# Reordering the first FFN1 group, two transposes, output copies and one unit's loads in a fused retention and FFN kernel

## The chip, the cores and the metric

One core of one Trainium2 chip. The metric is the device time of one execution in microseconds (us), lower is better. Where a mean granted TensorE clock matters it is given as a share of full speed.

## The reference, cut to what matters

```python
scores = scale * np.matmul(q, k.transpose(0, 1, 3, 2))     # 8 batches, 8 heads, 576 x 64
ret = scores * Dmat                                        # decay gamma_h ** (i - j), causal
attn = np.matmul(ret, v)                                   # -> x, 4608 tokens x 512
h = x @ w_in                                               # 512 -> 2048
g = np.where(h > 0.0, h, np.exp(np.minimum(h, 0.0)) - 1.0) # ELU
out = g @ w_out                                            # 2048 -> 512
```

## The kernel before

The engines go by short names: PE does the matmuls (TensorE), DVE is VectorE, ACT ScalarE, POOL GpSimd. A line such as L349 is a line of the kernel whose profile is shown; in a changed kernel the same code can stand a few lines lower.

Tokens are cut into 36 units of 128, and units into groups: the first group is units 0 to 2, then single units 3, 4 and 5, then larger groups. For a unit, `turn` transposes its queries and keys on PE (until unit 12; later ones by DMA) and copies them out on DVE and ACT; `scores` multiplies them; `masks` applies the causal mask on DVE; `inter`, `state` and `intra` (together the product) make the unit's output, and `put_x` copies it out of PSUM on DVE into the FFN input `xt`. FFN1 and FFN2 are the matmuls with `w_in` and `w_out`. For a group, FFN1 makes 16 tiles (for a single unit four share a PSUM bank, and "tile" then means the four). Each tile `ph` goes through three engines before its PSUM bank is free: `e` (exp, ACT), `m` (POOL), `g` (DVE).

PSUM, the memory that PE writes its results to, is the tight resource. The Trainium skill ("PSUM — Partial Sum Buffer", Specifications (TRN2)) gives 8 banks of 512 fp32 values per partition. This kernel uses all 8: 3 for `ph` (`h`), 1 for `pm` (`m`), 2 for scores and transposes (one two-bank tile, tag `sc`), 1 for products (`o`), 1 for the state.

```python
    def turn(u, bank=None, keys_on_v=False):
        ...
            else:
                both = ps_s.tile([P, 2, 2, HP, P], BF16, name="tr", tag="sc")   # two banks, one tile
                ps = [both[:, c, 0] for c in range(2)]
            ...                                                                 # 8 transposes on PE
            nc.vector.tensor_copy(t[:, c_v], ps[c_v])
            nc.scalar.copy(t[:, 1 - c_v], ps[1 - c_v])

    def stretch(u, ahead=True):            # the steady state, from unit 5 on
        ...
        scores(u + 1); inter(u); state(u); intra(u)      # shortened
        last = GROUPS[group_of[u][0]][-1] == u
        if last:
            put_x(u)
        if ahead:
            masks(u + 1)
        if not last:
            put_x(u)
        state_out(u)

    def finish(n=0):                       # puts the g's that are n slots old on DVE
        while late and late[0][0] <= slot[0] - n:
            _, gt_, ph, m, _ = late.pop(0)
            nc.vector.scalar_tensor_tensor(gt_, ph, 0.0, m, ALU.max, ALU.min)

    def tick():                            # after every FFN1 tile and every quarter of an FFN2 tile
        slot[0] += 1
        finish(3)
    ...
    load_w_in(1)                           # POOL issues these loads, in this order
    scale_v(1)
    load_qk(3)
    load_v(3, queue=nc.gpsimd)
    scale_v(2)
    load_w_in(2)
    load_w_in(3)
    load_w_out(0, 0, 8)
    load_w_out(0, 8, 16)
    load_w_out(1, 0, 16)
    dummy(2)
    for u in range(2):
        scores(u)
        masks(u)
        ...
        dummy(3)                           # keeps PE at work while it waits
        turn(u + 1, h, True)
        product(u)
        dummy(2)
    ...
    for n in range(2):
        ffn1_part(0, n, 0, 2)              # tiles 0 to 3 of units 0 and 1, ahead of unit 2
    product(2)
    for n in range(2, 4):
        ffn1_part(0, n, 0, 2, m if n == 3 else None)
    for n in range(4):
        ffn1_part(0, n, 2, 3)              # their part for unit 2
        f1(0, n)                           # e, m; g three slots later
    for n in range(4, 16):
        f1(0, n, m if n % 4 == 3 else None)
        if n == 5:
            turn(3)
        if n == 7:
            scores(3)
            masks(3, 0)
            scale_v(3)
        if n == 8:
            masks(3, 1)
        if n == 10:
            product(3)
    for n in range(4):
        f1(1, n, m if n == 3 else None)
        if n == 0:
            load_v(4, nc.vector)
        if n == 1:
            load_qk(4)
    finish()
    ...                                    # then FFN2 of units 0 to 3 in halves, turns 4 to 6
```

In these traces each engine runs its instructions in the order of the program text. The build adds the waits between engines.

## Time and profile before

| | before |
|---|---|
| time, median of 6 runs | 316.31 us (315.92 to 316.67) |
| span of the profiled run | 314.4 us |
| PE busy | 306.8 us, 98% |
| DVE, ACT, POOL busy | 55%, 42%, 64% |

The page of the kernel before: its busy times and the chain that ended last.

```profile
span 314.4 us, 7538 instructions
PE 306.8 (98%) x3020; PEld 173.9 (55%) x3020; DVE 172.7 (55%) x279; ACT 131.0 (42%) x243; POOL 200.9 (64%) x288
...
PE 89%; DVE 3%; DMA 3%; POOL 2%; issue 1%; ACT 0%; DVEq 0%; POOLq 0%; ACTq 0%
```

PE bounds the kernel and hardly ever stops. What can still be removed is in the view of waits of PE (columns: total us, times, longest):

```profile
PE dum L407 <- DVE warm L120: 1.2, 1, 1.2
PE ph L349 <- DVE g L316: 1.2, 1, 1.2
PE tr L194 <- DMA qkn<-in_k_dram: 0.8, 1, 0.8
PE pmh L390 <- DVE g L316: 0.3, 1, 0.3
PE sc L210 <- DVE rv L83: 0.2, 1, 0.2
PE tr L194 <- DVE pt L222: 0.2, 1, 0.2
```

This view hides the ends of matmuls that are still in the pipeline, so waits below read larger. They are start-to-start times of neighbouring matmuls minus the time the moving columns take: 1.33 us at 20.63 (FFN1 tile 4 of the first group waits for tile 0's bank), 0.44 at 37.8 (an FFN2 half waits for a bank), 0.31 at 57.55 and 0.33 at 69.91 (turns 7 and 9 wait for a mask), 0.24 at 113.34.

The stretch of the first group in the PE timeline of the kernel before (columns: start, length, engine, line, operation, tiles; in brackets idle time and what ended it):

```profile
20.63 1.46 PE L349 MATMUL ph<-xt,w_in_sb 128*128 128x384 bf16 x8 [1.16 <-DVE g L316]
21.93 0.61 PE L194 MATMUL tr<-ident,qkn 128*128 128x128 bf16 x8
22.38 1.46 PE L349 MATMUL ph<-xt,w_in_sb 128*128 128x384 bf16 x8
23.77 0.42 PE L210 MATMUL sc<-qkT 64*64 64x128 bf16 x16
24.12 2.14 PE L349 MATMUL ph<-xt,w_in_sb 128*128 128x384 bf16 x12
26.19 0.41 PE L238 MATMUL o<-qkT,sb 64*64 64x128 bf16 x8
```

After the one wait at 20.63, turn 3 (`tr`), FFN1 tiles, scores (`sc`) and product (`o`) follow without a gap. The same view of DVE and ACT has turn 3's copies at 22.58 to 23.00 (DVE) and 23.03 to 23.62 (ACT): the second starts 0.03 us after the first, although ACT was free from 22.68.

### The profile page before, as it was taken

To read this page: it belongs to the slowest core of one execution; us is meant where nothing else is said; L and a number is where in the kernel's file an instruction comes from. 1 tells how busy PE (TensorE), PEld (TensorE's weight loads), DVE (VectorE), ACT (ScalarE), POOL (GpSimd) and SP (SyncE) were. 2 spreads that over 40 slices of the span, in tenths; PEclk is the share of its full clock that TensorE was granted. 3 is DMA by queue.
4 is the path that set the end of the run, shared out by engine and by line. 5 is a ranking of instruction groups with operands and counts; after the bars stand their busy time and mean duration, and the time that the engine had idled before them with its cause. 6 is when DMAs were issued, how large, how long until landed. Compare 5 with 4: busy or idle time off the path is not lost.

```text
span 314.4 us, 7538 instructions
## 1 busy us (share of the span) xinstructions
PE 306.8 (98%) x3020; PEld 173.9 (55%) x3020; DVE 172.7 (55%) x279; ACT 131.0 (42%) x243; POOL 200.9 (64%) x288
## 2 busy tenths in 40 slices
PE   8889999999999999999999999999999999999995
PEld 3466888777665555555455444444444444444444
DVE  4658434757765656656655655555555555434300
ACT  4446314345434444343444444344444444344411
POOL 7977993968987788697777666766664433333300
PEclk9999999999999999999999999999999999999999
DMA  9999999996999999999999999999996200000111
GB/s 155 191 206 198 159 215 191 189 151 58 132 120 197 132 121 185 142 113 189 105 166 116 133 134 133 136 134 133 136 133 85 67 35 35 34 33 33 69 67 68
DMA packets 149235, 39.55 MB, mean 126 GB/s; under 512 B 137616, under 2 KB 145168, under 8 KB 149200
## 3 DMA queue, kind: packets, MB, share of 16 engines
q0 software_dynamic: 79264, 13.64, 56.7%
q1 hardware_dynamic: 67920, 23.14, 39.0%
q10 hardware_dynamic: 2016, 2.29, 2.3%
q8 instruction: 23, 0.38, 0.5%
q14 instruction: 12, 0.10, 0.1%
HBM read 36.70 MB, written 9.44 MB: 147 GB/s over the span
## 4 chain that ended last, share of the span: by engine, by line
PE 89%; DVE 3%; DMA 3%; POOL 2%; issue 1%; ACT 0%; DVEq 0%; POOLq 0%; ACTq 0%
PE ph L349 38%; PE pm L374 33%; PE pmh L390 5%; PE sc L210 4%; DMA w_in_sb<-in_moe_w_in_dram 3%; PE o L272 3%; PE st L255 2%; PE o L238 2%; PE dum L407 2%; PE tr L194 2%; DVE pt L222 1%; DVE g L316 1%; DVE xt L285 1%; POOL qkn L94 1%; POOL m L356 1%
## 5 line engine op out<-in xcount | busy, mean ns | idle before, releaser
L356 POOL TENSOR_SCALAR m<-e 128x512 bf16<-128x512 f32 (+1 forms) x156 | 90.9, 586 | 94.2 <-ACT e L354 91.9
L349 PE MATMUL ph<-xt,w_in_sb 128*128 128x512 bf16 (+3 forms) x816 | 143.2, 313 | 1.4 <-DVE g L316 1.2
L316 DVE SCALAR_TENSOR_TENSOR g<-ph,m 128x512 bf16<-128x512 f32 (+1 forms) x156 | 99.6, 647 | 80.8 <-POOL m L356 79.4
L354 ACT ACTIVATE e<-ph 128x512 f32<-128x512 f32 (+1 forms) x156 | 87.7, 565 | 125.0 <-PE ph L349 123.4
L374 PE MATMUL pm<-w_out_sb,g 128*128 128x512 bf16 x496 | 125.6, 379 | 0.0
L349 PEld LDWEIGHTS <-w_in_sb 128*128 128x128 bf16 x816 | 69.8, 98 | 54.8 <-issue 2.1
L374 PEld LDWEIGHTS <-g 128*128 128x128 bf16 x496 | 47.8, 98 | 53.1 <-issue 0.3
L222 DVE TENSOR_TENSOR pt<-sc,mask 128x1024 bf16<-128x1024 f32 (+1 forms) x37 | 44.1, 1192 | 18.7 <-PE sc L210 18.4
L175 POOL TENSOR_TENSOR vn<-rv,gk 128x512 bf16<-128x512 f32 x36 | 37.6, 1044 | 1.9 <-ACT qkT L196 1.1
L94 POOL DMA_DIRECT2D qkn<-in_q_dram x39 | 35.1, 900 | 0.0
L94 POOL DMA_DIRECT2D qkn<-in_k_dram x39 | 33.4, 857 | 0.1
L285 DVE TENSOR_TENSOR xt<-o,gx 128x512 bf16<-128x512 f32 x36 | 24.7, 685 | 15.2 <-PE o L272 15.1
L381 ACT COPY ot<-pm 128x512 f32<-128x512 f32 x31 | 18.2, 586 | 14.5 <-PE pm L374 14.4
L264 ACT CAST sb<-st 128x256 bf16<-128x256 f32 x32 | 11.9, 372 | 18.0 <-PE st L255 15.2
L390 PE MATMUL pmh<-w_out_sb,g 128*128 128x256 bf16 (+1 forms) x176 | 18.5, 263 | 0.3 <-DVE g L316 0.3
L390 PEld LDWEIGHTS <-g 128*128 128x128 bf16 x176 | 15.7, 98 | 2.3 <-issue 0.4
L210 PEld LDWEIGHTS <-qkT 64*64 64x64 bf16 x576 | 9.2, 106 | 13.5 <-issue 11.2
L210 PE MATMUL sc<-qkT 64*64 64x128 bf16 x576 | 15.0, 222 | 0.3 <-DVE rv L83 0.2
L272 PE MATMUL o<-pt,vn 128*64 128x128 bf16 x288 | 14.3, 221 | 0.0
L238 PE MATMUL o<-qkT,sb 64*64 64x128 bf16 (+1 forms) x256 | 12.3, 214 | 0.0
L395 DVE COPY oth<-pmh 128x256 f32<-128x256 f32 (+1 forms) x6 | 2.4, 402 | 16.2 <-PE pmh L390 16.2
L196 ACT COPY qkT<-tr 128x512 bf16<-128x512 bf16 x12 | 7.0, 584 | 9.8 <-DVE qkT L195 3.7
(41 smaller groups left out, 93.3 us busy)
## 6 DMA issues: line engine op xcount, KB each, us to landing
rv<-in_v_dram SPq DMA_DIRECT2D x31, 256.0 KB, 5.1
out_dram<-ot SPq DMA_DIRECT2D x27, 256.0 KB, 2.3
qkn<-in_q_dram POOLq DMA_DIRECT2D x31, 128.0 KB, 5.4
qkn<-in_k_dram POOLq DMA_DIRECT2D x31, 128.0 KB, 5.4
w_in_sb<-in_moe_w_in_dram POOLq DMA_DIRECT2D x4, 512.0 KB, 9.6
out_dram<-oth ACTq DMA_DIRECT2D x9, 128.0 KB, 4.3
w_out_sb<-in_moe_w_out_dram POOLq DMA_DIRECT2D x2, 512.0 KB, 13.7
w_out_sb<-in_moe_w_out_dram POOLq DMA_DIRECT2D x1, 1024.0 KB, 18.7
```

The costliest lines, as they stand in the source:

```text
L94: nc.gpsimd.dma_start(kns[u][p0 : p0 + n, c], (q, k)[c][b, :, s0 : s0 + n, :].rearrange("h p d -> p h d"))
L175: nc.gpsimd.tensor_tensor(n, rv, gk[:, u % R].unsqueeze(2).to_broadcast([P, H, D]), ALU.mult)
L210: nc.tensor.matmul(sc[j * 64 : (j + 1) * 64, i, hp], t[r, 1, hp, j * 64 : (j + 1) * 64], t[r, 0, hp], start=(hp == 0), stop=(hp == HP - 1) ...
L222: nc.vector.tensor_tensor(pts[u][:, s].rearrange("p i h t -> p (i h) t"), scs[u][:, s].rearrange("p i h t -> p (i h) t"), m.unsqueeze(1).t ...
L272: nc.tensor.matmul(o[i * D : (i + 1) * D, hp], vns[u][:, h], pts[u][:, i, hp], start=(u % R == 0 and hp == 0), stop=(hp == HP - 1), skip_g ...
L285: nc.vector.tensor_tensor(xts[g][:, :, i * P : (i + 1) * P], os_[u], gx[:, :, s0 : s0 + P], ALU.mult)
L316: nc.vector.scalar_tensor_tensor(gt_, ph, 0.0, m, ALU.max, ALU.min)
L349: nc.tensor.matmul(ph[:, i * n : (i + 1) * n], w_in_sb[:, j, f : f + P], xts[g][:, j, :n], start=(j == 0), stop=(j == KJ - 1), skip_group_ ...
L354: nc.scalar.activation(e[:, w], ph[:, w], AF.Exp)
L356: nc.gpsimd.tensor_scalar(m[:, w], e[:, w], -1.0, 1.0, ALU.add, ALU.mult)
L374: nc.tensor.matmul(pm, gts[g, ft][:, it * P : (it + 1) * P], w_out_sb[:, ft], start=(ft == 0), stop=(ft == NFT - 1))
L390: nc.tensor.matmul(pm, gts[g, ft][:, it * P : (it + 1) * P], w_out_sb[:, ft, c0:c1], start=(ft == 0), stop=(ft == NFT - 1),)
```

## The change

Its intent: the idle 1.33 us at 20.63 is filled by lending the two score banks to FFN1 tiles 4 and 5 of the first group, so unit 3, which needs those banks, moves later (its turn and scores by two tiles, its product by one). Bank `m` goes to other tiles too (`n % 4 == 1` instead of 3). Output copies that follow a mask go one slot later, so a `g` runs first and frees a bank. Unit 4's loads no longer stand before the last `m`'s of group 1. Turns 7 and 9 go one slot later, when their mask has ended.

```diff
@@ stretch
-            put_x(u)
+            outputs.append(u)
@@
+    outputs = []
+
     def tick():
         slot[0] += 1
         finish(3)
+        while outputs:
+            put_x(outputs.pop(0))
@@ first group
-    for n in range(4):
+    two = ps_s.tile([P, 2, 512], FP32, name="ph2", tag="sc")
+    phs[0, 4], phs[0, 5] = two[:, 0], two[:, 1]
+    for n in range(6):
         ffn1_part(0, n, 2, 3)
         f1(0, n)
-    for n in range(4, 16):
-        f1(0, n, m if n % 4 == 3 else None)
-        if n == 5:
+        if n in (1, 3):
+            ffn1_part(0, 4 + n // 2, 0, 2)
+    for n in range(6, 16):
+        f1(0, n, m if n % 4 == 1 else None)
+        if n == 6:
+            scale_v(3)
+        if n == 7:
+            finish(1)
             turn(3)
-        if n == 7:
+        if n == 9:
             scores(3)
             masks(3, 0)
-            scale_v(3)
-        if n == 8:
+            finish(1)
             masks(3, 1)
-        if n == 10:
+        if n == 11:
             product(3)
     for n in range(4):
-        f1(1, n, m if n == 3 else None)
+        f1(1, n, m if n == 1 else None)
         if n == 0:
             load_v(4, nc.vector)
-        if n == 1:
-            load_qk(4)
+    load_qk(4)
     finish()
@@ events of the steady state
-            events += [(due[u], 3, u + 2), (at(0.5), 1, u + 2)]
+            events += [(due[u], 3, u + 2), (at(0.7 if u in (5, 7) else 0.5), 1, u + 2)]
```

## The prediction

> **What bounds the kernel.** TensorE: the page gives PE 306.8 us busy of 314.4 (98%), clock fully granted; PE is 89% of the chain of waits that ended last. The Trainium skill ("Perfetto Trace Analysis", Identifying the Most-Contended Engine) warns that matmul busy share is no measure of headroom, so I took start-to-start times of neighbouring matmuls from the timeline and subtracted the usual spacing (0.162 us for 384 columns, 0.056 for 128). Removable waits, none after 150 us:
> - 20.63 us: 1.33, tile 4 of group 0 waits for the first eviction (DVE g) to free a bank
> - 37.80: 0.44, an FFN2 half waits for a g whose POOL step m stood behind unit 4's DMA issues
> - 54.43: 0.3, scores of unit 6 wait for copies (not touched)
> - 57.55, 69.91: 0.26, 0.28, turns (transposes) of units 7 and 9 wait for a mask in the score banks
> - 100.07, 113.34, 121.25, 136.14: about 0.2 each, FFN1 waits for g.
> This change can remove at most about 2.5 us, under 1%.
>
> **Outside the first group.**
> - Unit 4's issues after the four m's: -0.44. Its keys and queries land about 0.5 us later than 39.4; turn 4 is at 41 to 43, so no new wait.
> - Turns 7 and 9 one slot (0.87 us) later: -0.5 together. 2.2 us to their scores remain; a turn needs 1.75.
> - Output copies (0.69 us) behind the next g: only units not last in their group change. Of the late waits only 113.34 has that order (mask, xt, g): -0.24. At 100 and 121 xt precedes the mask and stays; 136 waits on POOL issues.
> Sum -1.2.
>
> **First group, walked by hand with trace durations** (e 0.49; m and g paced 0.475, g 0.56 long; vn 1.04; a turn's copies 0.42 DVE, then 0.59 ACT; masks 0.69 per half). Tiles 4 and 5 add 1.32 us of ready matmuls (8x0.109+8x0.056), so tile 6 starts at 20.63 just as the first g ends: that wait vanishes. But:
> - turn 3 uses the same score banks and must await g of tile 5. Six g's from 20.02 end near 22.95; PE is there at 21.93: new wait 1.0.
> - POOL does vn of unit 3 (22.8 to 23.8) before m of tile 7; g 7 ends near 24.9, and turn 3's copies now stand behind it: ready 25.9. PE wants the scores at 24.75: wait 1.2.
> - the second mask half is behind g 8 and g 9, ending near 28.7; PE wants it at 28.2: 0.5.
> Tile 12 then starts near 29.1 instead of 27.65: +1.45. Perhaps more: the ACT copy of these turns always starts 0.03 us after the DVE copy, though they use different banks of the two-bank tile; if the same serialisation holds between tile 4's exp and tile 5's last matmuls, add 0.5. But the order looks hand-tuned, so something in my walk may be slack; I take +1.3.
>
> **Prediction.** 316.04 + 1.3 - 1.2 = 316.1 us, range 314.8 to 317.2. Faster by over 2%: 0.01; within 2%: 0.98; slower: 0.01.
>
> **What would show it.** PE "tr" waits on DVE g and PE "sc" on the ACT copy between 21 and 27 us; "ph on DVE g" at 20.6 gone; no waits in the FFN2 half and at turns 7 and 9; 113 gone, 100, 121, 136 still there (shifted); group 1 starts 1 to 2 us after 30.3.
>
> **What would make it wrong.** If turn 3 and its scores find banks and copies ready (POOL faster than 0.475 there), the gain is 2.5 us: 313.6. If the two-bank tile is serialised, or later loads delay turn 4 or 5: 317 or more.

## The result, and the profile after

| | before | after |
|---|---|---|
| time, median of 6 runs | 316.31 us (315.92 to 316.67) | 318.47 us (317.67 to 319.21) |
| span of the profiled run | 314.4 us | 316.9 us |
| PE busy | 306.8 us | 303.7 us |

The ratio is 1.0066, with a 95% interval of 1.0047 to 1.0085: slower by 2.1 us, clear of noise though under 2%. A ratio is the mean time of one kernel's fast runs over that of the other's fast runs of the same rounds, so it is not quite the ratio of the medians quoted. The after trace has records of 2992 of 3028 matmuls, against all 3020 of before, so its lower busy time is no gain.

The page after, and its waits of PE:

```profile
span 316.9 us, 7519 instructions
PE 303.7 (96%) x2992; PEld 173.8 (55%) x3028; DVE 172.9 (55%) x279; ACT 131.0 (41%) x243; POOL 200.7 (63%) x288
...
PE 89%; DVE 3%; DMA 3%; issue 1%; POOL 1%; ACT 1%; DVEq 0%; POOLq 0%; ACTq 0%
```

```profile
PE tr L194 <- DMA qkn<-in_k_dram: 1.7, 2, 1.5
PE dum L411 <- DVE warm L120: 1.2, 1, 1.2
PE sc L210 <- ACT qkT L196: 1.1, 1, 1.1
PE ph L353 <- DVE g L316: 0.9, 2, 0.7
...
PE ph L335 <- ACT e L358: 0.6, 1, 0.6
PE tr L194 <- DVE g L316: 0.6, 1, 0.6
...
PE o L272 <- DVE pt L222: 0.3, 1, 0.3
```

The wait of `pmh` is gone, and so is the long one of `ph` in the first group. In their place stand four waits in the first group: `ph` on tile 4's exp, `tr` on `g`, `sc` on the ACT copy, `o` on the mask. From start to start they are 0.81, 0.78, 1.25 and 0.45 us. (The two waits of `ph` on `g` that are listed, 0.9 us, come later, at 60.02 and 74.60: FFN1 tiles ahead of the two turns that were moved.) They are seen in the PE timeline of the kernel after:

```profile
21.71 0.38 PE L335 MATMUL ph<-xt,w_in_sb 128*128 128x128 bf16 x4 [0.64 <-ACT e L358]
21.93 1.46 PE L353 MATMUL ph<-xt,w_in_sb 128*128 128x384 bf16 x8
24.01 0.61 PE L194 MATMUL tr<-ident,qkn 128*128 128x128 bf16 x8 [0.62 <-DVE g L316]
24.45 1.46 PE L353 MATMUL ph<-xt,w_in_sb 128*128 128x384 bf16 x8
27.00 0.42 PE L210 MATMUL sc<-qkT 64*64 64x128 bf16 x16 [1.08 <-ACT qkT L196]
...
29.74 0.38 PE L272 MATMUL o<-pt,vn 128*64 128x128 bf16 x7 [0.28 <-DVE pt L222]
```

The queue behind the scores, in the timelines of POOL, then DVE, of the kernel after:

```profile
23.89 1.04 POOL L175 TENSOR_TENSOR vn<-rv,gk 128x512 bf16<-128x512 f32 x1
24.90 0.51 POOL L360 TENSOR_SCALAR m<-e 128x384 bf16<-128x384 f32 x1
```

```profile
25.44 0.56 DVE L316 SCALAR_TENSOR_TENSOR g<-ph,m 128x384 bf16<-128x384 f32 x1 [0.93 <-POOL m L360]
25.91 0.41 DVE L195 COPY qkT<-tr 128x512 bf16<-128x512 bf16 x1
```

Read it from the scores at 27.00 backwards: they wait for the ACT copy (26.36 to 26.94), that for the DVE copy (25.91), that stands on DVE behind `g` of tile 7, which waits for `m` of tile 7 (24.90), which stands on POOL behind `vn` of unit 3 (23.89). In the kernel before, turn 3's copies stood behind no such `g`.

**The ledger.** The same landmarks can be found on PE in both traces: the start of the scores of a unit. Their differences (after minus before, us) say where time was lost.

| scores of unit | before, at | after minus before | what lies since the last one |
|---|---|---|---|
| 2 | 14.53 | +0.50 | the start, the same program in both |
| 4 | 45.32 | +1.97 | first group +1.91, wait at 37.8 -0.44 |
| 7 | 60.79 | +2.42 | turn 7: +0.45 |
| 9 | 73.07 | +2.51 | turn 9: +0.09 |
| 16 | 117.75 | +2.28 | output copies: -0.23 |

From there to unit 35 the difference stays at 2.28; another 0.22 comes after the last matmul. This end is not chance: in all nine traces with the new first group the last DRAIN of DVE, one of the closing steps, starts 3.32 to 3.36 us after the last matmul, in the other five 2.96 or 2.97, and the span ends 0.2 us later. So it comes with the first-group part; why is open. The first group's +1.91 is 1.97 - 0.50 + 0.44, as the wait at 37.8 falls in the same interval. So four parts of the change make 1.91 - 0.44 + 0.54 - 0.23 = 1.78 us, and with the end 2.00. The start of this pair of profiled runs adds 0.50, and differs from run to run (see the last experiments).

### The profile page after: what moved, and what is told of

Read it like the earlier page. It is cut to its first block, busy times and chain, and to the rows that moved or that the text cites. A ratio compares the mean times of both kernels' runs of the same rounds, so it can differ in the third digit from the quotient of the medians.

```text
span 316.9 us, 7519 instructions
## 1 busy us (share of the span) xinstructions
PE 303.7 (96%) x2992; PEld 173.8 (55%) x3028; DVE 172.9 (55%) x279; ACT 131.0 (41%) x243; POOL 200.7 (63%) x288
## 4 chain that ended last, share of the span: by engine, by line
PE 89%; DVE 3%; DMA 3%; issue 1%; POOL 1%; ACT 1%; DVEq 0%; POOLq 0%; ACTq 0%
PE ph L353 37%; PE pm L378 33%; PE pmh L394 6%; PE sc L210 4%; PE o L272 3%; DMA qkn<-in_k_dram 3%; PE st L255 2%; PE o L238 2%; PE tr L194 1%; DVE g L316 1%; DVE pt L222 1%; POOL qkn L94 1%; ACT e L358 1%; PE ph L335 1%; DVE xt L285 0%
## 5 line engine op out<-in xcount | busy, mean ns | idle before, releaser
L353 PE MATMUL ph<-xt,w_in_sb 128*128 128x512 bf16 (+3 forms) x792 | 140.9, 312 | 1.9 <-DVE g L316 0.9
L378 PE MATMUL pm<-w_out_sb,g 128*128 128x512 bf16 x478 | 122.8, 379 | 1.5 <-issue 0.8
L353 PEld LDWEIGHTS <-w_in_sb 128*128 128x128 bf16 x808 | 68.9, 98 | 54.3 <-issue 1.5
```

What stands on the lines that cost most here:

```text
L353: nc.tensor.matmul(ph[:, i * n : (i + 1) * n], w_in_sb[:, j, f : f + P], xts[g][:, j, :n], start=(j == 0), stop=(j == KJ - 1), skip_group_ ...
L378: nc.tensor.matmul(pm, gts[g, ft][:, it * P : (it + 1) * P], w_out_sb[:, ft], start=(ft == 0), stop=(ft == NFT - 1))
```

## The experiments

Main theory: the loss is the ledger's, that is, waits made by the order of queues in the first group and by the two later turns. Rivals: the start and its loads are the loss; the output copies cost in every stretch; lending the score banks is itself the whole loss.

All kernels were correct. "Landmarks" are differences from the profiled run of before, at the scores of units 2, 4, 9 and 16. Each kernel was timed in 6 runs, beside 11 of before. The intervals of e2, e3, e4, e6 and e8 include 1: their times alone decide nothing, and the reading rests on the landmarks of one trace each. These repeat from kernel to kernel: turns 7 and 9 cost 0.45 and 0.09 in each of the four traces that move them.

### One part alone

**e1_group**: only the first-group part (with its `m if n == 1`). Edit: the hunks "first group" of the diff, with `load_qk(4)` left at `n == 1`.

> The kernel before with only the first-group part of the change. Main theory (the first group alone costs more than the whole loss of 2.2 us: three new waits, at the last part of tile 5 on tile 4's exp, at turn 3 on DVE g, at the scores of unit 3 on the ACT copy): +1.9 us of before, scores of unit 3 on PE about 2.7 us later than before's 23.77 apart from an offset of the start, and the wait at 37.8 still there. Rival (the loss lies in the start of the run and in its loads, the order of the first group only shows it): within 0.5 us of before.

Measured: 322.65 us (319.63 to 323.67), before 316.75; ratio 1.0160 (1.0121 to 1.0199). Landmarks -0.43, +3.22, +3.22, +3.23. This missed both expectations, and the trace of the fastest run (319.63) says why: the FFN2 half at 37.8 now waits 2.19 us instead of 0.44, as this line of its PE timeline shows.

```profile
39.27 0.92 PE L390 MATMUL pmh<-w_out_sb,g 128*128 128x256 bf16 x7 [2.02 <-DVE g L316]
```

With the new order of banks the second half needs tile 2 of group 1, whose `m` stood behind unit 4's loads. Of the 3.65 us between the landmarks of units 2 and 4, 1.75 are this wait; the first group is 1.90, as in the ledger. The rest is in the timed runs: their granted clock was 0.989 (three runs, over 323 us) and 0.995 (two, near 322), against 0.999 in the profiled one. The rival "the start and its loads" fell: this start was earlier than before's.

**e9_group_loads**: e1 with the loads moved as in the change.

```diff
-        if n == 1:
-            load_qk(4)
+    load_qk(4)
     finish()
```

> The kernel of e1 (before with the new first group) with unit 4's loads issued after the fourth tile. Main theory (the new bank order makes an FFN2 half need g of tile 2 of group 1 earlier, so with the old loads the wait at 37.8 grew from 0.44 to 2.19, and such a wait also let the granted clock fall in most of e1's timed runs, 0.989 to 0.995 against 0.999 in the profiled one): no wait there, +1.5 us of before, clocks of the timed runs at 0.998 or more. Rival (the low clocks of e1 come from the first group itself or from the chip): clocks again near 0.99 and +5 us.

Measured: 317.92 us (317.79 to 319.43), before 316.67; ratio 1.0041 (1.0016 to 1.0066); clocks 0.998 to 1.0 in all six. Landmarks -0.02, +1.46, +1.46, +1.46; first group +1.92. So e1's excess in the trace was the wait at 37.8. That the same wait lowered the clock of its timed runs fits, but is not shown: e1's profiled run had the wait and kept its clock, and some runs of before read 0.993 to 0.995 too. The two parts of the change belong together: the new bank order needs the later loads.

**e2_turns**: only the turns of units 7 and 9 later.

```diff
-(at(0.5), 1, u + 2)
+(at(0.7 if u in (5, 7) else 0.5), 1, u + 2)
```

> The kernel before with only the turns of units 7 and 9 one slot later. Main theory (a turn one slot earlier hides FFN1's wait for its bank under its transposes; later, both are paid one after the other): +0.45 and +0.09, together +0.5 us, with a new wait of an FFN1 matmul on DVE g near 58.0. Rival (as predicted: both waits vanish): -0.5 us.

Measured: 317.19 us, before 316.75; ratio 1.0007 (0.9978 to 1.0036). Landmarks -0.16, -0.23, +0.31, +0.32, with +0.45 at turn 7 and +0.09 at turn 9, to the hundredth the ledger's. Here is turn 7 in the PE timeline of before, then of e2:

```profile
56.38 1.03 PE L374 MATMUL pm<-w_out_sb,g 128*128 128x512 bf16 x4
57.55 0.61 PE L194 MATMUL tr<-ident,qkn 128*128 128x128 bf16 x8
58.05 1.05 PE L349 MATMUL ph<-xt,w_in_sb 128*128 128x128 bf16 x16
```

```profile
56.15 1.03 PE L374 MATMUL pm<-w_out_sb,g 128*128 128x512 bf16 x4
57.83 1.05 PE L349 MATMUL ph<-xt,w_in_sb 128*128 128x128 bf16 x16 [0.65 <-DVE g L316]
58.72 0.61 PE L194 MATMUL tr<-ident,qkn 128*128 128x128 bf16 x8
```

In before, the transposes wait 0.31 us and run for 0.45, and by then the bank of the next FFN1 tile is just free (its `g` ended at 58.00 and the tile starts at 58.05). In e2 the FFN1 tile comes first, and waits 0.82 us for that bank; the transposes are paid after it. The turn had been hiding the other wait.

**e3_copies**: only the output copies later (the hunks of `stretch` and `tick`).

> The kernel before with only the output copies one slot behind the masks. Main theory: -0.24 us, from the wait at 113.3 alone, all later stretches of equal length. Rival (the deferred copies cost in each stretch, or at the tail, where the run of after lost 0.2 us more): +0.2 us or more.

Measured: 316.56 us, before 316.75; ratio 0.9991 (0.9961 to 1.0021). Landmarks -0.05, +0.64, +0.64, +0.41: the wait at 113.3 goes (-0.23), nothing else changes in the steady state. The rival fell; the end of the span is not longer either (+0.01). The +0.69 before unit 4 is not from the edit, which touches nothing there: the wait of FFN1 tile 4 was 2.03 us in this run instead of 1.33. What sets it is shown by the chain of waits of the kernel before (columns: start, length, what):

```profile
8.59 9.42 DMA w_in_sb<-in_moe_w_in_dram
18.01 0.28 issue
18.30 1.15 POOL w_out_sb L109
19.44 0.02 issue
19.46 0.54 POOL m L356
```

The first `m` stands on POOL behind the issue of the last `w_out` load, and that waits for a `w_in` load to land. In e3 this issue ended at 20.09 instead of 19.44, 0.8 us after the exp of tile 0 had ended. So this wait differs from run to run with the loads.

**e4_loads**: only unit 4's loads later (the edit of e9, on before).

> The kernel before with only unit 4's key and query loads issued after the fourth tile of group 1. Main theory: the wait at 37.8 goes, turn 4 does not wait: -0.44 us. Rival (the later loads push the loads behind them, and turns 4 to 6 or the state of unit 5 wait): 0 or more.

Measured: 316.45 us, before 316.75; ratio 0.9985 (0.9956 to 1.0014). Landmarks -0.31, -0.49, -0.37, -0.37. Between turn 3 and the scores of unit 4 it gains 0.43 us, and no wait is left at 37.8. It gives back 0.12 within the transposes of unit 9, which did not recur in e10.

**e10_loads_copies**: e4 with the edit of e3.

> The kernel before with only the two parts that gained, unit 4's loads later and the output copies one slot later. Main theory: the two gains add, -0.44 and -0.24, together -0.7 us. Rival (one of them only moves a wait that the other meets): -0.4 or less.

Measured: 316.04 us (315.37 to 317.01), before 316.62; ratio 0.9977 (0.9955 to 0.9999). Landmarks +1.38, +0.89, +0.89, +0.66: after its start it gains 0.43 at the loads and 0.23 at the copies. The gains add.

### The first group taken apart

Each of these keeps the edits of the one before it.

**e5_both_first**: the changed kernel, with the last matmuls of tiles 4 and 5 both ahead of tile 4's exp.

```diff
     for n in range(6):
-        ffn1_part(0, n, 2, 3)
+        if n < 4:
+            ffn1_part(0, n, 2, 3)
+        if n == 4:
+            ffn1_part(0, 4, 2, 3)
+            ffn1_part(0, 5, 2, 3)
         f1(0, n)
```

> The changed kernel with one edit: the last matmuls of tiles 4 and 5 both ahead of the exp of tile 4. Main theory (the wait of 0.8 us at tile 5 is a wait for tile 4's exp, a read of the other bank of the same two-bank tile; it also delays the whole chain behind it): that wait goes, and the first group costs 1.4 us more than before's instead of 1.9, 0.5 us less than the changed kernel; the waits at turn 3 (0.8) and at its scores (1.2) stay. Rival (the wait is for the bank's data, or has no effect because POOL's pace sets the end): the wait stays at about 0.8, or goes and the scores of unit 3 are no earlier.

Measured: 317.92 us (317.60 to 318.28), before 316.67; ratio 1.0032 (1.0010 to 1.0054). Landmarks +0.53, +1.50, +2.04, +1.81: first group +1.41, 0.50 less than the changed kernel. The wait on the exp is gone; the one at turn 3 has grown from 0.78 to 1.26 and that at the scores is 1.08, where I had expected both to stay as they were:

```profile
23.72 0.61 PE L194 MATMUL tr<-ident,qkn 128*128 128x128 bf16 x8 [1.09 <-DVE g L316]
26.53 0.42 PE L210 MATMUL sc<-qkT 64*64 64x128 bf16 x16 [0.91 <-ACT qkT L196]
```

So PE did wait for ACT to read one bank of the two-bank tile before it wrote the other: a dependence on the tile, not on the data. The kept traces rule out a rival for the turns, whose two copies also write one tile (`qkT`): in turns 0 to 2 of before, with the two halves in separate PSUM tiles, ACT's copy does not wait for DVE's (12.85 against 13.28 us in turn 2).

**e6_queue**: `vn` of unit 3 behind turn 3, and no flush of the `g`'s ahead of it.

```diff
-        if n == 6:
-            scale_v(3)
         if n == 7:
-            finish(1)
             turn(3)
+            scale_v(3)
```

> The kernel of e5 with one more edit: vn of unit 3 on POOL behind turn 3 instead of ahead of m of tile 7, and no flush of the g's ahead of the copies of turn 3. Main theory (the 1.2 us wait of the scores is the queue order vn, m 7, g 7, copy, copy): that wait goes, the scores of unit 3 follow tile 9 at once, and the second mask half becomes the gate (0.5 to 0.7 us); FFN1 tile 12 about 1.0 us earlier than in e5, the first group at +0.4 us of before's. The wait at turn 3 for g of tile 5 stays. Rival (the score banks, lent to tiles 4 and 5, are the cause of both waits): the scores still wait about 1 us.

Measured: 317.24 us (316.76 to 318.36), before 316.67; ratio 1.0013 (0.9989 to 1.0037). Landmarks +0.60, +0.60, +1.14, +0.90: first group +0.44, 0.97 less than e5. The scores no longer wait; turn 3 still does (1.27 us), and so does the product for the mask (0.45). The rival fell. In its PE timeline:

```profile
23.79 0.61 PE L194 MATMUL tr<-ident,qkn 128*128 128x128 bf16 x8 [1.10 <-DVE g L316]
25.63 0.42 PE L210 MATMUL sc<-qkT 64*64 64x128 bf16 x16
```

**e8_all_orders**: both mask halves together, turns 7 and 9 in their old slots.

```diff
             masks(3, 0)
-            finish(1)
             masks(3, 1)
@@
-at(0.7 if u in (5, 7) else 0.5)
+at(0.5)
```

> The kernel of e7 with turn 3 in the score banks again (as in e6), all else as in e7: it leaves the lent banks as the one difference from e7. Main theory: turn 3 waits about 1.2 us for g of tile 5 and then runs while w_in would have been waited for anyway (0.76 us in e7), so it loses the 0.45 us of the turn itself and what the wait exceeds: 0.8 to 1.0 us slower than e7, within 0.6 us of before, no wait at scores or masks. Rival (the order of the queues alone was the loss): as fast as e7.

Measured: 315.97 us (315.53 to 317.00), before 316.62; ratio 0.9979 (0.9955 to 1.0003). Landmarks +0.12, -0.37, -0.36, -0.60: first group -0.05, no better than before's. Turn 3 still waits:

```profile
23.31 0.61 PE L194 MATMUL tr<-ident,qkn 128*128 128x128 bf16 x8 [1.10 <-DVE g L316]
```

**e7_turn_in_o**: e8 with turn 3 in the bank of the products, which is free then.

```diff
+            if bank == o:
+                both = ps_o.tile([P, 2, HP, P], BF16, name="tr", tag="o")
+                ps = [both[:, c] for c in range(2)]
@@
-            turn(3)
+            turn(3, o)
```

> The kernel of e6 with turn 3 in the free bank of the products instead of the score banks, both mask halves together, and the turns of units 7 and 9 back in their old slots. Main theory: no wait at turn 3 and none at the masks; what is left is a wait of FFN1 tile 8 for the third quarter of w_in, which lands near 23.0 to 23.3; first group 0.6 us shorter than before's, kernel 0.6 + 0.44 + 0.24 = 1.3 us faster than before: 315.0 where before has 316.3. Rival (DVE and POOL pace bound the first group in any order): no better than before.

Measured: 315.37 us (315.02 to 316.19), before 316.67; ratio 0.9956 (0.9931 to 0.9981), faster than before by 1.4 us. Landmarks -0.09, -1.07, -1.07, -1.30: first group -0.54. In its PE timeline turn 3 follows tile 7 at once, and the only wait is for weights:

```profile
21.84 0.61 PE L197 MATMUL tr<-ident,qkn 128*128 128x128 bf16 x8
23.04 1.47 PE L356 MATMUL ph<-xt,w_in_sb 128*128 128x384 bf16 x8 [0.59 <-DMA w_in_sb<-in_moe_w_in_dram]
24.45 0.42 PE L213 MATMUL sc<-qkT 64*64 64x128 bf16 x16
```

Against e8 the lent banks cost 0.49 us, about half of what I expected (0.8 to 1.0). It is a net figure: e7 pays 0.76 us for the weights, a wait that turn 3's own wait hides in e8. So the first group's loss has four parts, measured by undoing them one after the other, in this order only (in another the shares might differ): the exp ahead of tile 5's matmuls 0.50, the order of POOL's and DVE's queues 0.97, the flush between the mask halves 0.49, the lent banks at turn 3 0.49. They sum to 2.45, which is the way from e7 (-0.54) to the changed kernel (+1.91).

**e11_w_in_first**: e7 with the third quarter of `w_in` issued ahead of unit 3's loads, and unit 3 two tiles later again.

```diff
+    load_w_in(2)
     load_qk(3)
     load_v(3, queue=nc.gpsimd)
     scale_v(2)
-    load_w_in(2)
@@ turn, scores, product of unit 3
-        n == 7, n == 9, n == 11
+        n == 9, n == 11, n == 13
```

> The kernel of e7 with the third quarter of w_in issued ahead of unit 3's loads, and turn, scores and product of unit 3 two tiles later. Main theory (the last wait in the first group, 0.76 us in e7, is for that quarter): that wait goes or shrinks below 0.2, 0.5 us faster than e7, unless unit 3's loads, now later by some 3 us, make turn 3 wait. Rival (POOL's pace of m and DVE's of g bound the group): no faster than e7, new waits of FFN1 on DVE g.

Measured: 315.79 us (314.91 to 316.05), before 316.62; ratio 0.9960 (0.9940 to 0.9979). Landmarks +1.44, -0.34, -0.34, -0.57: the first group is -1.34, 0.8 better than e7 in the trace, and no wait on `w_in` is left. The times don't show this gain: the start took 1.44 us more in the profiled run, and two of the six runs had a clock of 0.995 (the expectation for e12 below says three, a misreading). The next point looks at that start.

### The start and the granted clock

In e10 and e11 the profiled run itself caught the lower clock. This is the view of stretches of e10 (columns: window, its length, busy time and count of PE, PEld, DVE, ACT and POOL, then PEclk, DMA share, GB/s), and then of the kernel before:

```profile
8.00:11.50 3.50, 1.54 (x26) 0.89 (x26) 1.39 (x3) 1.72 (x4) 3.48 (x5) 1.00 1.88 172
11.80:15.00 3.20, 3.20 (x39) 1.85 (x29) 1.70 (x3) 0.59 (x1) 3.20 (x5) 0.50 1.30 204
```

```profile
8.00:11.50 3.50, 2.67 (x50) 1.44 (x47) 2.08 (x3) 2.67 (x5) 3.48 (x5) 1.00 1.92 173
11.80:15.00 3.20, 3.17 (x58) 1.82 (x55) 2.35 (x4) 0.96 (x2) 3.20 (x5) 1.00 1.27 205
```

In e10 PE waited 1.8 us for the keys of unit 1 and was busy for 1.54 of the 3.5 us from 8.0 to 11.5; the clock then stood at half for one stretch of 3.413 us. In before PE was busy for 2.67 us of the same window and kept its clock. The Trainium skill ("TensorE: Matmul & The Clock Gate", What's actually happening) has a free-running window of 3413 ns, and half the clock after an idle one. The length agrees exactly; the condition does not, since PE was not idle: in the 3.41 us before that stretch it was busy for 1.44. Nor does a wait of this size suffice: PE waited 2.19 us near 39 in the trace of e1 and 2.03 near 21 in that of e3, and both kept the full clock. What decides stays open. By estimate from the 3.413 us, one such stretch lowers the mean clock of a 315 us run to 0.995, two to 0.989, which are the readings of the longer runs of e1; in which place e1 lost it no profile shows.

**e12_fill_start**: e11 with more dummy matmuls in that wait.

```diff
-        dummy(3)
+        dummy(6 if u == 0 else 4)
         turn(u + 1, h, True)
```

> The kernel of e11 with three more dummy matmuls (0.65 us) ahead of the transposes of unit 1, which wait 0.8 to 1.8 us for that unit's keys, and one more ahead of those of unit 2. Theory (that wait, when long, lets the granted clock fall to half for one 3.41 us window near 12 us, as in the profiled runs of e10 and e11, which costs 1.4 us; three of six runs of e11 and some of all kernels had a clock of 0.993 to 0.995): no run below 0.998, the highest and lowest time within 1 us, median 315.2 or lower where before has 316.6. Rival (the lowered clock comes by chance or from elsewhere): clocks of 0.993 to 0.995 again in some runs, median no lower than e11's.

Measured: 315.15 us (314.74 to 315.90), before 316.43; ratio 0.9959 (0.9942 to 0.9975); clocks 0.999 to 1.0 in all six, the spread 1.16 us where I had expected at most 1. Two of the 11 runs of before beside it had 0.994, at 317.35 and 317.61 us. It fits the theory; six runs don't prove that the fall can no longer happen (in e8, without the extra dummies, all six read 0.998 or more as well). By ratio e12, e11 and e7 can't be told apart. All three beat both kernels.

## Why the prediction was wrong

The sum predicted was +1.3 - 1.2, about +0.1; the measured difference is +2.1 us, and 318.47 lies above the range. Point by point:

- **What bounds the kernel, and how little can be gained: right.** At most 2.5 us could be removed, as predicted; the best variants gained 1.3 to 1.4.
- **"Unit 4's issues after the four m's: -0.44": right**, -0.43 in e4 and e10, and turn 4 did not wait. I missed that the first group's new bank order depends on it (e1).
- **"Output copies ... -0.24": right**, -0.23, at 113 alone; the waits near 100 and 121 stayed.
- **"Turns 7 and 9 one slot (0.87 us) later: -0.5 together": this step failed.** It is +0.54, in the change and alone (e2). The waits at the turns (0.31 and 0.33) did go, but FFN1 waits of 0.82 and 0.41 came. I took the wait of the turn as time that vanishes and checked that its scores stay in time. I did not ask what the next instruction on PE would wait for when the turn is taken away from in front of it: the FFN1 tile, on a bank freed after the same mask on DVE. A difference of 1.0 us from the sum.
- **"First group ... I take +1.3": mechanism right, size wrong.** The waits at turn 3, at its scores and at the mask came where the walk put them, made by what the walk named (the queues in e6 and e8, the lent banks in e7). The walk gave +1.45; the serialisation of the two-bank tile was named as a possible 0.5 more and left out, and 0.15 was taken off because the order looked hand-tuned. The serialisation was real and cost 0.50 (e5); the group cost 1.91. 1.45 + 0.5 was the right sum for this pair of traces; before's wait at 20.63, which is part of it, reads 1.26 to 2.03 in the traces that keep the old first group.

Together: 1.91 instead of 1.3, and +0.54 instead of -0.5, make 1.65 us of the miss of 2.0 (+2.1 instead of +0.1). The longer end, for which the prediction had no term, makes 0.22 more, its cause open. The last 0.1 or so is within the noise of the times. (The time of 316.1 missed by 2.4, as its base of 316.04 was one run, 0.3 below the median of before.)

## What to carry to other kernels

Before an instruction is moved away from a wait, ask what stands behind it in its queue and what that waits for: the instruction and its wait may be covering another wait (here 0.31 us of waiting at turn 7 became 0.82 at an FFN1 tile). Lending a bank brings its whole release chain to the next user: follow that chain through every queue, with all that stands ahead in each (here a 1.04 us POOL operation ahead of one small `m`). A serialisation that the trace shows for one user of a multi-bank tile should be counted for another user of the same kind of tile, not held in reserve.

## What the Trainium skill lacked or had wrong

- "PSUM — Partial Sum Buffer", Specifications (TRN2), says ScalarE and VectorE can access PSUM in parallel as long as there is no bank collision. What it lacks is that a program may not get this for two banks of one tile: here the build made ACT's copy wait for DVE's (0.03 us after its end in each turn of before and after that used the two-bank tile), and PE's write for ACT's read (0.81 us at 21.71; gone in e5).
- "TensorE: Matmul & The Clock Gate", Back-to-back issue gap, gives 81 ns for N=128 and 131 ns for N=512 as the sustained spacing of pairs of weight load and matmul, and calls N / 2.4 + 2.5 ns an isolated figure. In this trace streams of such pairs ran at a median of 56 ns for 128 columns and 216 ns for 512: the isolated formula is the one that fits (the page itself also reports measured back-to-back gaps of 55.6 and 215.7 ns, so it is not at one with itself).
- The same page, HAM oscillation, puts the rule as no PE-idle gaps over about 3.4 us. In e10 a wait of 1.8 us, with PE busy for 1.54 of 3.5 us, was followed by 3.413 us at half clock; in e3 one of 2.03 us was not.
- "Perfetto Trace Analysis", Optimization Strategy (under Identifying Performance Opportunities), tells to look for the gap before an instruction and its releaser. None of the pages I read says that one gap can hide the next in the same queue; here 0.54 us of the loss came from that.
